# Weight and mask loads issued by SyncE or ScalarE, and a new order of work, in a kernel of attention and two expert layers

## The chip, the cores and the metric

One core of a Trainium2 chip runs the program. The metric is device time in microseconds from start to end of one execution; three runs give a median. One more execution was taken with the hardware profiler; all rows below come from that one.

## What is computed

Two batches of 8 heads, 768 positions, head size 64. Every position belongs to the cluster (of 16) whose centroid it is most alike; a query sees only keys of its own cluster. The attention output goes, as 1536 rows of 512, through two expert layers.

```python
q_assign = np.argmax(np.einsum('bhsd,hcd->bhsc', q_n, c_n), axis=-1)      # q_n, k_n, c_n: normalized
k_assign = np.argmax(np.einsum('bhsd,hcd->bhsc', k_n, c_n), axis=-1)
mask = q_assign[:, :, :, None] == k_assign[:, :, None, :]
scores = np.where(mask, scale * np.matmul(q, k.transpose(0, 1, 3, 2)), -1e9)
attn = softmax(scores); x = np.matmul(attn, v)        # -> (1536, 512)
h = x @ w_in                                          # 512 -> 2048
g = np.where(h >= 1, h, np.where(h <= -1, 0.0, (h + 1) ** 2 / 4.0))
x = g @ w_out                                         # 2048 -> 512
out = ((x @ w1) * (x @ w2)) @ w3 @ w_out2             # 512 -> 1024 -> 512
```

## The kernel before

Matmuls run on pairs of float32r numbers: each operand is split into a high part (a copy, L352 on ACT or L354 on DVE) and a low part (a subtraction, L357 on DVE or POOL), and three products are added (tiles of weights: `wf` whole, `whl` or `wh` split). The weights come as float64, seen as pairs of 32-bit words in a staging tile `w64`; L1107 and L1111 (ACT) and L1115 and L1121 (DVE) turn them into float32 in `wf`. Weights that batch 1 needs again are stored in DRAM (`wd`, L1126) and fetched from there.

The work has three stages. **Batch 0's attention** (about 0 to 200 us): keys and queries are loaded into `kq0` (L513), projected on the centroids (L539), turned into a mask of 16 rows per head (L555 to L590), and the mask rows are copied behind each head's keys and queries in `kq2` (the mask fill, L728). Beside it the product of the last two weight matrices is made (L1169) and kept in DRAM as `wp`. **The middle** (about 200 to 470 us): batch 1's attention beside batch 0's pass through the expert layers (L1239, 12 matmuls to a group of one weight tile and half the rows). **The last third**: batch 1's pass, for which sums and differences of blocks are made (L1403) so that seven products (L1492) do the work of eight.

Attention goes by units (two heads of one batch) and half units of 6 score tiles. A score tile is four matmuls (L859) into a bank `sc`; a maximum (L867, DVE), a bias (L872, POOL), the exponential (L880, ACT); then it must be transposed. In batch 0 PE does that (L897); in batch 1, except for two tiles, a high and a low half go to a `phl` buffer (L352 or L354, then L357) and a transposing DMA from SP's queue (L927) writes them to `pt`. There are two banks and two `phl` buffers in batch 1: a bank is free once the low half is made, a `phl` buffer once the DMA has landed. When the six tiles of a half unit are in `pt`, 36 matmuls (L976; L968 in batch 0) multiply them with the values.

The order is not found by a scheduler at run time. Every piece of work is declared with `add(name, {engine: cost}, due, ...)`, with alternatives such as `{"ACT": .., "DVE": (.., LATE)}`; a search made offline has chosen the order and the engine of each piece, and the string `ORDER` (two letters to a piece, 3035 pieces) holds the result. Each engine gets its instructions in that order and executes them in it. Instructions that issue DMAs stand in the same order: SP's are those of pieces declared with the engine "DMA", ACT's stand between its activations. Costs and due times in `add` are used by the search alone.

Before the change all 152 weight fetches (`load`, L1101, L1103 and L1413) and batch 0's seven mask fills (L728, two DMAs each) are issued by ACT; everything else by SP. In the middle stage `w64` has three buffers; a fetch into one waits until L1121 has read it.

Of the kernel before, what the change touches and what calls it, by code (L numbers as in the profile page):

```python
# [38 lines left out]
    "###*#,#0#%#(#8$V%X%[#.#2#4$0$.$6$2$X%e%h$8$:#F%V%b$<%c%q%k%m$Z$_$a%i%]$>$c$4$H#D$J#R#g%y&,:m:|%_#Z$%$(;0;>$@"  # L39
    "$B$F%|&#$e$L$g$N$]$q$i$k$s$P$m$o%s%u$u$w#>:q:o$,#J#L#B#_#:$D%o;#$R#q%w;L;%$T;4;2)u)w)y#y#c#<#N#T$*#u#V$y$|)|"  # L40
    ";@;B:s;(:u:x:y*4*(***,*6;**#*%#P#]*@*B%#;P;]*.*8*:*D*F;N#k#o#m#6#e#|#s#X*0*<*2*>;6;-;8;m;/&&;;;<;a*L*H$#*N*P"
    "<#*X*Z*];D;F&)*J*R#i#w#H#@#a*u;_;c;R*_*e<4;T;I;J+(*T*V*a*c*w+4+6+*;e;g;q;V<D<(*m;o;s*y*|+#+@&1*g+8+:;u+,+.<T"
    "+0+<&6<%&*+B+&+2<H*i*l*o&2&:+L+N;w;z+X+Z<*<,*r<.*s%>&5&9<X;X;Z+D&G+F+P+R+H+T<c+>+]+_+u&/&<+J+a+V+c;j;k%%+w+y"
    ",(,4,6&E,*<8<6<F<:<V+|<J<L+e<s<<&I<N%@&K<?,8,:,,,.<@+m,#,%<g,<,0,2,>,L,@,B,D+g,N,P<w=*,X,Z,]&N<e<i,F,R<k<Z<]"
    "<n<`<a<p=:;|<0<2,_,T,H,J,V&>+i+l,a,u,w,y<u<y<|=.=J=#%(,c&P-(-*-,+o<B<Q<R,|-#,e,g=>=,=<=0+q=X&@-.&B-4-6-8=@=B"
    "&M=2=D=i-%-:=5=6+s<q=%=(-0-2-<-@&c-B-D=N=L=P=R&S=U=V=Z=]=_&T=y->>0=k-F-L-X-Z-]-N,m,i=a,l-P=m=o=q=s=d=e>@-R-_"
    ">P=|>#>2&Y-H-u-w,o-e-g>%-J>a,q=8=G=H>(,s>4-a-T-V.(.*-d&Z>6-y=g=v=w>o-|>*>-&b>8>:%*>D&i&V&_>T&k&v>B>F>H&^>K>M"
    "&e.#.%-m-i.4.6.,..?#>s.@-k>e.0.3&o.8.B&m.D&g-o>.>=>>.:?4>R>V>c>q&s.L.N.P.X.<>X>Z.Z%B?(-q>N.F>g>i.R.>?F>u>l>w"
    "?%?*>z?,.H>n>~.T.]._.a.J?V.u.V-s>]/(/4?.?0/*/,.c?i&z(&?@>_/@/B.w?2?B?D&w($(-%,?8&q?y.m?Z?J/.?6?H?X&|((%D/6.y"
    ".|/#/8/:/<?m/%?:?<?>?L?]/D?N?_?k?o?a(..e/0/2?q/>%.%0%2%4%F?P.g?R/F?s/L/N/H/P?c@,@2@#@B?|%6%H/J(*/R@T?T?e?g%J"  # L50
    "%L/X%8%:%</Z.i.k.o?u@%@(@6@4@8/T0(/V/]/_.q.s@:?w@.@0@e/a/c/u@*0*0,@D@F@<@w@X/w@>0./y/|@i@V@g@N%N0406@H@J@L@Z"
    "/m/e@]00%P%R%T@kA.@`@m@o0#0%@|02080:@@@P@b@yA#A%@R@q0@0<0L0>/g/i0XA@AP/k0N0P0B0DA:/o0u0w0yA)@c@s@u0Z0R0F0T/q"
    "0H0KA*A2A0A40|0W0]0_0e0gA6ADAcABA,A<A>0a0cA8As/s1((0(2ARATAFAHAJ1*1,1.1#Ag(4(61416AVAXAe1%AMAiAkA]AZ0mAuAnAp"
    "100i1X1Z12B%Aw0kB,0o181:1@1L(:1N1P1B1D(=(8(>ANA_AaAy(AA|B#1R0q1<1]1T1>1F(B1_B/(E(H(M1e1g(NAqB(B*1H1J1V1a1d0s"
    "1i1kBJ2*2,(F(J2.Bi2022C.B01u1w1y1|(Z(P24(R1m(TBMBO1o2#2%26(V(X2(1q1sB2B4282:2<B6CLCkBkBn2FB82H2>2AD02B2DB>BP"
    "B]B@BBBDC02J2L2O2PC2B:B<BRCNCQB_BbBTBF2T2V2X2ZBHC4C6FLC82]BVD>2cBcBY2eB[2R2_2aBoBq2g2i2kBtC:C<BfBgC>B|C#C&Bu"
    "FPBw2m2oCn3%C@CB3(D2C(CD3*3,CF3436By383.30Fe3:CHCpCKC_CRCT3B3<(_C+CaCWC,3>(hD53D(]32CX3F3@CcCe(bFiD@(c(eG#DL"
    "DZ3H3K2y3P3R3TD#D%CZC]D(3V3LD*3NChCqCs3Y3Z3]CuD,DBD6D:3mD<DOCwD9DQD^Cz3_(jDiG(3a3c3e2qE.3gELD`2s3o(t3q3sDDDG"
# [81 lines left out]
def cluster_attention_moe_kernel(  # L140
# [115 lines left out]
    def G():  # L256
        return blk_tile("G")
# [401 lines left out]
    def dma_of(b):  # L659
        return nc.sync.dma_start if b else nc.scalar.dma_start  # L660
# [52 lines left out]
    def kq_fill(u, h):  # L713
        def fn(e):
            b, j = units[u]
            hd = 2 * j + h
            dma = dma_of(b)
# [1040 lines left out]
```

## Time and profile before

| | |
|---|---|
| median of 3 runs | 721.11 us (721.01 to 721.91) |
| the profiled execution: its time | 723.58 us |
| the profiled execution: its span | 721.5 us |
| PE, DVE, ACT, POOL busy | 699.0, 618.2, 468.2, 290.9 us |
| mean granted clock of TensorE | 0.998 |
| moved by DMA | 122.36 MB: 62.18 MB on SP's queue (q1), 59.42 MB on ACT's (q10) |

PE is the engine to look at: its idle time in each stage, and for each wait the instruction that ended it. A wait is put down to what came last. SP and ACT issue DMAs; the DMA share is the mean busy share of 16 DMA engines, and it can read above 1 where packets of several transfers overlap.

### The profile page before, as it was taken

How to read it: one execution, taken by the hardware profiler on the slowest of the kernel's cores; microseconds unless marked ns; L12 is line 12 of the kernel's file. 1: busy time of each engine (PE TensorE's matmuls, PEld its weight loads, DVE VectorE, ACT ScalarE, POOL GpSimd, SP SyncE). 2: the span in 40 equal slices, each digit the busy share in tenths (PEclk: the TensorE clock that was granted, in tenths of full speed). 3: DMA queues.
4: the chain of work that ended last, by engine and by line, in shares of the span. 5: the costliest groups of instructions: out<-in, count | busy, mean ns of one | idle time of the engine just before them, and what ended most of it. 6: DMA issues, size and time to landing. Idle time of an engine off the chain costs nothing.

```text
span 721.5 us, 11974 instructions
## 1 busy us (share of the span) xinstructions
PE 699.0 (97%) x4173; PEld 631.2 (87%) x4173; DVE 618.2 (86%) x1080; ACT 468.2 (65%) x872; POOL 290.9 (40%) x359
## 2 busy tenths in 40 slices
PE   5999999999999999999999989999999999999998
PEld 2876776677799999999899988999999999999997
DVE  7999999989889998898999879568878869999940
ACT  7998999779786877977787656236764525543211
POOL 3344433221253454455321312317573426387510
PEclk9999999999999999999999999999999999999999
DMA  8357867777989998998989898673222122121122
GB/s 313 124 179 232 278 208 251 249 250 219 231 190 199 216 226 220 215 243 160 267 216 247 208 155 202 155 219 113 59 88 74 45 73 61 52 80 59 58 70 77
DMA packets 125644, 122.36 MB, mean 170 GB/s; under 512 B 83792, under 2 KB 92432, under 8 KB 125584
## 3 DMA queue, kind: packets, MB, share of 16 engines
q1 hardware_dynamic: 103024, 62.18, 36.2%
q10 hardware_dynamic: 22560, 59.42, 26.3%
q8 instruction: 33, 0.54, 0.3%
q14 instruction: 27, 0.22, 0.1%
HBM read 75.79 MB, written 22.28 MB: 136 GB/s over the span
## 4 chain that ended last, share of the span: by engine, by line
PE 71%; DVE 11%; DMA 7%; ACT 6%; issue 3%; POOL 1%; ACTq 0%; SPq 0%; DVEq 0%; POOLq 0%
PE mo L1239 33%; PE sc L1239 6%; PE sc L859 6%; PE sc L1492 6%; PE mo L1492 4%; PE mo L1169 3%; PE av L976 3%; PE sc L897 2%; PE av L968 2%; DMA pt<-phl 2%; PE av L1239 2%; DMA wf<-wp 2%; PE av L1492 1%; DVE tv L1403 1%; ACT P L880 1%
## 5 line engine op out<-in xcount | busy, mean ns | idle before, releaser
L1239 PE MATMUL mo<-X,whl 128*128 128x384 f32 x912 | 167.9, 338 | 0.0
L1239 PEld LDWEIGHTS mo<-X,whl 128*128 128x128 f32 x912 | 159.5, 189 | 1.7 <-DVE G L354 0.3
L1239 PE MATMUL mo<-G,whl 128*128 128x384 f32 x672 | 124.1, 339 | 0.0
L357 POOL TENSOR_TENSOR whl<-wf,whl 128x512 fp32r<-128x512 f32 x62 | 81.2, 1310 | 97.9 <-DVE whl L354 42.2
L1239 PEld LDWEIGHTS mo<-G,whl 128*128 128x128 f32 x672 | 118.2, 188 | 1.0 <-issue 0.6
L867 DVE TENSOR_REDUCE nm<-sc 128x1 f32<-128x768 f32 x96 | 90.0, 950 | 5.7 <-PE sc L859 5.2
L872 POOL TENSOR_SCALAR nm<-nm 128x1 f32<-128x1 f32 x96 | 34.6, 360 | 146.9 <-DVE nm L867 141.5
L352 ACT ACTIVATE whl<-wf 128x512 fp32r<-128x512 f32 x71 | 44.4, 627 | 46.0 <-PE mo L1239 26.2
L1111 ACT ACTIVATE w<-w,down 128x512 uint32<-128x512 uint32 x72 | 54.5, 763 | 8.4 <-DMA pt<-phl 3.9
L859 PE MATMUL sc<-k,q 128*128 128x512 f32 (+1 forms) x192 | 54.1, 363 | 5.7 <-DVE phl L357 2.6
L880 ACT ACTIVATE sc<-sc,nm 128x768 f32<-128x768 f32 x46 | 40.0, 870 | 20.6 <-POOL nm L872 19.8
L1115 DVE SCALAR_TENSOR_TENSOR wf<-wf,w 128x512 uint32<-128x512 uint32 x72 | 51.0, 714 | 2.3 <-ACT wf L1107 1.7
L1107 ACT ACTIVATE wf<-w 128x512 f32<-128x512 f32 x72 | 47.4, 671 | 6.3 <-POOL whl L357 3.6
L1121 DVE SCALAR_TENSOR_TENSOR wf<-w,wf 128x512 uint32<-128x512 uint32 x72 | 50.3, 702 | 1.1
L880 ACT ACTIVATE P<-sc,nm 128x768 f32<-128x768 f32 x50 | 44.8, 898 | 9.9 <-DVE nm L867 5.6
L859 PE MATMUL sc<-kq 80*128 80x512 f32 (+1 forms) x192 | 49.7, 341 | 0.0
L357 DVE TENSOR_TENSOR phl<-sc,phl 128x768 f16<-128x768 f32 x46 | 43.8, 952 | 3.2 <-ACT phl L352 2.6
L357 DVE TENSOR_TENSOR whl<-wf,whl 128x512 fp32r<-128x512 f32 x50 | 35.1, 704 | 10.1 <-ACT whl L352 9.4
L859 PEld LDWEIGHTS sc<-k,q 128*128 128x128 f32 x192 | 31.4, 190 | 13.5 <-ACT pt L352 4.2
L897 PEld LDWEIGHTS sc<-ident,P 128*128 128x128 f32 x300 | 33.5, 140 | 10.1 <-ACT P L880 7.2
L1239 PE MATMUL sc<-G,whl 128*128 128x384 f32 x228 | 42.0, 339 | 0.0
L897 PE MATMUL sc<-ident,P 128*128 128x128 f32 x300 | 39.7, 275 | 2.3 <-ACT P L880 2.1
(235 smaller groups left out, 1462.0 us busy)
## 6 DMA issues: line engine op xcount, KB each, us to landing
wf<-wd ACTq DMA_DIRECT2D x64, 256.0 KB, 2.8
w<-in_w_out_dram ACTq DMA_DIRECT2D x24, 512.0 KB, 4.2
wd<-wf SPq DMA_DIRECT2D x48, 256.0 KB, 3.4
w<-in_w3T_dram ACTq DMA_DIRECT2D x16, 512.0 KB, 4.0
w<-in_w_in_dram ACTq DMA_DIRECT2D x16, 512.0 KB, 4.5
w<-in_w_dram ACTq DMA_DIRECT2D x16, 512.0 KB, 5.1
wp<-wf SPq DMA_DIRECT2D x16, 256.0 KB, 3.0
wf<-wp ACTq DMA_DIRECT2D x16, 256.0 KB, 3.2
```

Of the source, the lines that this page charges most:

```text
L352: nc.scalar.activation(out=out, in_=in_, func=AF.Copy)
L357: (nc.gpsimd if e == "POOL" else nc.vector).tensor_tensor(out=out, in0=a, in1=b, op=ALU.subtract)
L859: nc.tensor.matmul(ps[:, n], q[0:n_rows, q0:q0 + 128], k[0:n_rows, n], start=first, stop=not first)
L867: nc.vector.tensor_reduce(out=nm, in_=T[("sc", b), s], axis=AX.X, op=ALU.max, negate=True)
L880: nc.scalar.activation(out=new(("P", b), s).rearrange("p n s -> p (n s)") if by_pe(s) else T[("sc", b), s], in_=T[("sc", b), s], func=AF.E ...
L897: nc.tensor.transpose(T[("sc", b), s][:, c], p[:, c], ident)
L1107: nc.scalar.activation(out=T["wf", i], in_=T[w64, i].bitcast(F32)[:, :, 1], func=AF.Abs, scale=float(2.0 ** -112))
L1111: nc.scalar.activation(out=lo, in_=lo, func=AF.Identity, scale=float(2.0 ** -29 - 2.0 ** -41), bias=down)
L1115: nc.vector.scalar_tensor_tensor(out=w, in0=w, scalar=3, in1=T[w64, i][:, :, 0], op0=ALU.logical_shift_left, op1=ALU.bitwise_or)
L1121: nc.vector.scalar_tensor_tensor(out=w, in0=T[w64, i][:, :, 1], scalar=0x80000000, in1=w, op0=ALU.bitwise_and, op1=ALU.bitwise_or)
L1239: nc.tensor.matmul(acc, w[:, a, k4 * 128:(k4 + 1) * 128], rhs(c, k4), start=(first and k4 == 0 and n == 0), stop=(last and k4 == 3 and n = ...
L1492: nc.tensor.matmul(ps, lhs(av, a, k), rhs(bv, c, k), start=k == 0 and n == 0, stop=k == 1 and n == 2,)
```

## The change

Each weight fetch and each mask fill of batch 0 is now a piece that may stand on SP or on ACT, with costs for the search, and `ORDER` is another one. In the code:

```diff
-    def dma_of(b):
-        return nc.sync.dma_start if b else nc.scalar.dma_start
+    def dma_of(e):
+        return nc.sync.dma_start if e == "DMA" else nc.scalar.dma_start
...
-                    ("k2", u, h), {"DMA": 1.95} if b else {"ACT": 0.3}, p - 6.0, kq_fill(u, h),
+                    ("k2", u, h), {"DMA": 1.95} if b else {"ACT": 0.3, "DMA": (0.9, 8.0)}, p - 6.0, kq_fill(u, h),
...
-                nc.scalar.dma_start(out=new("wf", i), in_=src)
+                (nc.sync if e == "DMA" else nc.scalar).dma_start(out=new("wf", i), in_=src)
...
-            add(("wl", i), {"ACT": 0.2}, t - 14.0, load, list(needs) + W_AFTER[i:i + 1], [(w64, i)], behind="w64", moves=((0.46, 1.8),))
+            add(("wl", i), {"ACT": 0.2, "DMA": (0.5, 8.0)}, t - 14.0, load, list(needs) + W_AFTER[i:i + 1], [(w64, i)], behind="w64", moves=((0.46, 1.8),))
...
-    "iqi#i%iXitiuiZi]i_iwiyi|"
+    "iiiZi^i_i#iqisi%iuiwiyi|"
```

L1101 (fetches of float64 weights) and L1413 (batch 1's fetches) change as L1103 does. By the new table 100 of the 152 fetches and all seven mask fills are on SP: 34 of 44 fetches before the first transposing DMA of the middle stage, 22 of the 47 up to the last one (before the change 46 stood there), 44 of the 61 behind it. The first fetches of keys (`kT`, by head pair) come in the order 0, 2, 1, 3, after 1, 0, 2, 3 before; the printed rows do not tell the pairs apart. The pieces are the same 3035, and PE's sequence is nearly the same.

Where batch 1's last unit but one is done, SP's queue had transposes of two half units (`pt`, from the two `phl` buffers) beside stores of weights (`wd`):

```order
L927 DMA_TRANSPOSE pt1_97<-phl1_112 128x12x128
L1017 DMA xd_84<-tmp_4370 128x384
L927 DMA_TRANSPOSE pt2_98<-phl0_111 128x12x128
L1126 DMA wd_85<-wf_4441 128x512
L927 DMA_TRANSPOSE pt2_98<-phl1_112 128x12x128
L1126 DMA wd_85<-wf_4374 128x512
L1126 DMA wd_85<-wf_4495 128x512
L927 DMA_TRANSPOSE pt0_96<-phl0_111 128x12x128
L927 DMA_TRANSPOSE pt0_96<-phl1_112 128x12x128
```

and now has, for the same six score tiles:

```order
L927 DMA_TRANSPOSE pt1_97<-phl1_112 128x12x128
L1101 DMA w641_114<-in_w12_dram 128x1024
L1126 DMA wd_85<-wf_4312 128x512
L1126 DMA wd_85<-wf_4373 128x512
L1101 DMA w642_115<-in_w12_dram 128x1024
L927 DMA_TRANSPOSE pt2_98<-phl0_111 128x12x128
L927 DMA_TRANSPOSE pt2_98<-phl1_112 128x12x128
L1101 DMA w640_113<-in_w12_dram 128x1024
L1126 DMA wd_85<-wf_4413 128x512
L1126 DMA wd_85<-wf_4482 128x512
L1126 DMA wd_85<-wf_4528 128x512
L927 DMA_TRANSPOSE pt0_96<-phl0_111 128x12x128
```

The three fetches of `w12` into `w640` to `w642` stood on ACT; now a transpose has one or two of them ahead of it on SP.

On PE, at the same place, the score tile in bank `sc_1917` was followed by one group of L1239, the next score tile (bank `sc_1916`), another group, and then L976:

```order
L859 MATMUL sc_1917<-kq_105 128x512
L859 MATMUL sc_1917<-kq_105 128x256
L1239 MATMUL mo_1912<-X_2080,whl 128x384 x12
L859 MATMUL sc_1916<-k_99,q_102 128x512
L859 MATMUL sc_1916<-k_99,q_102 128x256
L859 MATMUL sc_1916<-kq_105 128x512
L859 MATMUL sc_1916<-kq_105 128x256
L1239 MATMUL mo_128<-X_2080,whl 128x384 x12
L976 LDWEIGHTS vn
```

and now (the banks are numbered 1913 and 1912):

```order
L859 MATMUL sc_1913<-kq_105 128x512
L859 MATMUL sc_1913<-kq_105 128x256
L1239 MATMUL mo_1907<-X_2086,whl 128x384 x12
L1239 MATMUL mo_1908<-X_2086,whl 128x384 x12
L1239 MATMUL mo_128<-X_2086,whl 128x384 x12
L976 LDWEIGHTS vn
```

Three groups and the 36 matmuls of L976 now stand ahead of the next score tile, `sc_1912`.

On DVE, in the last third, from the last y sum (L1274) to the last low half of `BX`, before:

```order
L1274 TENSOR_TENSOR Yp<-Yp,mo_128 128x384
L1403 TENSOR_TENSOR tt_4941<-Yp 128x384
L357 TENSOR_TENSOR X_75<-Yp,X_75 128x384
L1403 TENSOR_TENSOR Yp<-Yp,tt_4940 128x384
L357 TENSOR_TENSOR whl<-wf,whl 128x512
L357 TENSOR_TENSOR BX<-tt_4941,BX 128x384
L357 TENSOR_TENSOR BX<-Yp,BX 128x384
L1403 TENSOR_TENSOR tt_4942<-Yp 128x384
L357 TENSOR_TENSOR BX<-Yp,BX 128x384
L1403 TENSOR_TENSOR ws_4949<-wf 128x256
L1403 TENSOR_TENSOR ws_4950<-wf,ws_4948 128x256
L357 TENSOR_TENSOR BX<-tt_4940,BX 128x384
```

and now:

```order
L1274 TENSOR_TENSOR Yp<-Yp,sc_5174 128x384
L357 TENSOR_TENSOR whl<-wf,whl 128x512
L357 TENSOR_TENSOR X_75<-Yp,X_75 128x384
L1403 TENSOR_TENSOR tt_4945<-Yp 128x384
L357 TENSOR_TENSOR BX<-tt_4943,BX 128x384
L1403 TENSOR_TENSOR ws_4951<-ws_4950,wf 128x256
L357 TENSOR_TENSOR BX<-Yp,BX 128x384 x2
L357 TENSOR_TENSOR BX<-tt_4940,BX 128x384
```

Eleven instructions followed the y sum there, now eight do; one sum of weights (`ws`) has moved behind.

## Rows read from the trace of the kernel before

**Rows 1.** The page's totals: busy us, share of the span, instructions.

```profile
PE 699.0 (97%) x4173; PEld 631.2 (87%) x4173; DVE 618.2 (86%) x1080; ACT 468.2 (65%) x872; POOL 290.9 (40%) x359
```

**Rows 2.** Busy time of each engine by stage, granted clock, DMA share, GB/s.

```profile
0.00:200.00 200.00, 185.67 (x1126) 136.69 (x1127) 183.82 (x301) 173.74 (x295) 67.44 (x100) 1.00 0.73 231
200.00:470.00 270.00, 267.36 (x1660) 251.25 (x1659) 238.09 (x385) 187.86 (x343) 103.40 (x126) 0.99 0.90 207
470.00:722.00 252.00, 245.97 (x1391) 243.22 (x1389) 196.34 (x396) 106.56 (x236) 120.08 (x134) 1.00 0.26 81
```

**Rows 3.** Timeline of PE, 428 to 433: start, us, instruction, idle before.

```profile
428.52 2.29 PE L1239 MATMUL mo<-X,whl 128*128 128x384 f32 x12
432.97 1.01 PE L859 MATMUL sc<-k,q 128*128 128x512 f32 x2 [2.16 <-DVE phl L357]
```

**Rows 4.** The chain that ended last, 418 to 433: start, us, what.

```profile
417.98 12.90 DMA pt<-phl
...
430.97 0.97 DVE phl L354
...
432.97 1.65 PE sc L859 x4
```

**Rows 5.** The page's DMA issues: count, median us from issue to landing.

```profile
pt<-phl SPq DMA_TRANSPOSE x46, 4.2
```

**Rows 6.** The transposing DMA of L927 that was issued at 423.17, and its landing.

```profile
L927 SPq DMA_TRANSPOSE pt<-phl x1: 4213/4213/4213, 423.2 to 423.2; - x1
DMA to landing us min/median/max: 13.0/13.0/13.0
```

**Rows 7.** Timeline of ACT and its issues, 417 to 432.

```profile
417.82 0.83 ACTq L1101 DMA_DIRECT2D w<-in_w_dram  x2
...
426.79 4.50 ACTq L1101 DMA_DIRECT2D w<-in_w_dram  x2
431.33 0.75 ACT L1111 ACTIVATE w<-w,down 128x512 uint32<-128x512 uint32 x1 [3.92 <-DMA pt<-phl]
```

**Rows 8.** Stretches of 2 us as in rows 2: the granted clock is third from the end.

```profile
431.00:433.00 2.00, 0.03 (x1) 0.03 (x1) 1.97 (x3) 0.75 (x1) 0.00 (x0) 0.93 1.65 142
433.00:435.00 2.00, 2.00 (x6) 1.81 (x7) 1.86 (x4) 0.40 (x1) 0.58 (x2) 0.50 0.69 185
435.00:437.00 2.00, 2.00 (x10) 2.00 (x10) 1.77 (x3) 1.89 (x5) 0.65 (x1) 0.72 1.09 414
```

**Rows 9.** The third and fourth load of L513 and their landings.

```profile
L513 SPq DMA_DIRECT2D kq<-in_kT_dram x2: 431/432/432, 2.2 to 2.7; - x2
DMA to landing us min/median/max: 5.9/6.2/6.4
```

**Rows 10.** Timeline of PE and of DVE at the start.

```profile
8.25 1.51 PE L539 MATMUL sc<-kq,cT 128*32 128x384 f32 x8 [2.11 <-DMA kq<-in_kT_dram]
...
9.82 0.58 DVE L555 STREAM_TRANSPOSE P<-sc 128x384 f32<-128x384 f32 x1 [1.33 <-PE sc L539]
```

**Rows 11.** Waits of PE and of ACT, 20 to 200: us in total, times, longest.

```profile
PE sc L859 <- ACT pt L352: 2.2, 6, 0.7
PE sc L897 <- ACT P L880: 2.1, 4, 0.8
...
ACT whl L352 <- issue: 0.4, 1, 0.4
ACT wf L1107 <- issue: 0.3, 1, 0.3
```

**Rows 12.** The page's groups of instructions: the weight copies on ACT.

```profile
L352 ACT ACTIVATE whl<-wf 128x512 fp32r<-128x512 f32 x71 | 44.4, 627 | 46.0 <-PE mo L1239 26.2
```

**Rows 13.** Timeline of PE and of DVE, 622 to 630.

```profile
629.94 0.61 PE L1492 MATMUL mo<-BX,wh 128*128 128x384 f32 x2 [0.88 <-DVE BX L357]
...
622.42 0.54 DVE L1274 TENSOR_TENSOR Yp<-Yp,mo 128x384 f32<-128x384 f32 x1
...
627.58 0.97 DVE L1403 TENSOR_TENSOR ws<-wf 128x256 f32<-128x256 f32 x1
```

More of the change, by code (lines that the diff above doesn't have):

```diff
@@ L44 @@
[L44 to L58, printed above, removed]
@@ new lines @@
+    "+B+.*g*i*l+8+:+<<H<%+0+2<8;w<X+L+N;z+X+Z*o<*&>;g&2<,*r&;<.;X+D+F+P&9*s;Z;j;k<t&7+R+T+H+]+_+>&/&<+u+a+J+V,(,4"
+    "+c+m&F<6<F&D+w+y+|,#,6,8,*,,,:<:,.,<<J+e<L<N&5<V<<=+<Z&I<?<@,%<g,0,2,>,@,L,B,D+g<e<w=;,N,P,F,R,X,Z,],_<]<i<k"
+    ";|<0<2<n<p<`<a&K=J,H,T,J,V,a+i+l,u,w<u<y<|=#-(-*+o=X<B<Q%@&O<R=.=,=0,c,y,|-#=j=N=<=>+q&P-,&@&B,e,g-4-6-.=@=B"
+    "+s&S=2=D-%-8-:=L=P=5=6<q-0-2=%&c=]&L=R=T=z-@-<-B=m->=Z=k-L-X-N=W-P-D,m-F>1=(>A-Z-]-_>#,i,k=|=_=a&l&U=o=d=q=e"
+    ",o-H-a-u-w&W&t>Q>2-R-e-g=s=8>%=G=H-J,q>D-T-V&o-c&^.(.*>4.,>(>+>T,s>6-y-|=g=u&e>b&`>p%(=w>8>:>->B&X?#&[&b%B%*"
@@ new lines @@
+    ".4.6.8>F>H&j&n.#.%...:-i-k-m-o>J>L.0.@.3.B.D&v>.>=>R>V&g>>.L.N.P?4-q>e>c?(>q>s>X>Z.F.X.<.R.Z.].>>N?G>g>u>i?W"
+    "._>w.T.H?%?*>l?,>z>n.J.V>]>_?.>~?1.u.a/(/4.c?@?8&y&|/*-s/,&q?6/@.w/B/D?Z&w?H((/.?j?m?X.y.|?z(&?2?B?D(-($%,%D"
+    "/6/8/:.e?:?<?>?]?_.m?J?L/#/%@3/<?k?o/0/2/>?N?P?R?a?q%.%0%2%4@#/F%F?s/L/N%6%H/H/J@6?c?T?e@C%J%L/P/R@,(+@U@e/X"
+    "%8%:?u.g.i.k/Z/]?|.o(.@%@(@4/T0(@8@:?g?w@./V@*%</_.q.s/a/c@F@0@=@>@w/u/w/y0*0,@X@D@i/|040608/m0.000#@H@J%N%P"
+    "@V@g/e/g@Z@N%R@LA/AA%T0%020:@]@_@k@m@o@b@@@P@y@|A#0<0L0>0@0B/i/k0DA20N0P@q0F@RA%A(A*0R0X/oA0AQ0u0w0Z0]A:@c@s"
@@ L96 @@
+    "gTgCfefifmh%h*g>fggLh:h,g|fZh<h>g2gJhfhhhih.h1fohHhJfqgVgXhLh$fkfsgNhBh(h@h2fufwh6gZg_hNg]hkhpi)hqh8hsh4gPga"
+    "gigchDhmhTi*hXh[i3i5iDgeggi7i,i.i0hFh]i8huhPhVhRglh_hbhwgmhch|iGiHi>i;iOibiQici@iBiRhyilifiLiJinipigiTiViXi<"
+    "iiiZi^i_i#iqisi%iuiwiyi|"
 )
@@ L716, in fn @@
             hd = 2 * j + h
-            dma = dma_of(b)
+            dma = dma_of(e)
             kq2 = f(T[("kq2", b), (u, h)])
@@ L1100, in load @@
             if is64:
-                nc.scalar.dma_start(out=new(w64, i), in_=src.bitcast(U32).rearrange("p (n t) -> p n t", t=2))
+                (nc.sync if e == "DMA" else nc.scalar).dma_start(out=new(w64, i), in_=src.bitcast(U32).rearrange("p (n t) -> p n t", t=2))
             else:
-                nc.scalar.dma_start(out=new("wf", i), in_=src)
+                (nc.sync if e == "DMA" else nc.scalar).dma_start(out=new("wf", i), in_=src)
         def absv(e):
@@ L1151, in chunk @@
         else:
-            add(("wl", i), {"ACT": 0.2}, t - 12.0, load, needs, [("wf", i)], behind="wf", moves=((0.46, 1.05),))
+            add(("wl", i), {"ACT": 0.2, "DMA": (0.5, 8.0)}, t - 12.0, load, needs, [("wf", i)], behind="wf", moves=((0.46, 1.05),))
             last = ("wl", i)
@@ L1412, in load @@
             def load(e, i=i, n=n):
-                nc.scalar.dma_start(out=new("wf", i), in_=wd[n])
-            add(("wl", i), {"ACT": 0.2}, t - 16.0, load, [("wd", n)], [("wf", i)], behind="wf", moves=((0.46, 1.05),))
+                (nc.sync if e == "DMA" else nc.scalar).dma_start(out=new("wf", i), in_=wd[n])
+            add(("wl", i), {"ACT": 0.2, "DMA": (0.5, 8.0)}, t - 16.0, load, [("wd", n)], [("wf", i)], behind="wf", moves=((0.46, 1.05),))
             rows_.append(i)
```

85 lines of the change are left out of this document (44 added, 41 removed).

## The prediction, made before the result was known

> **What bounds the kernel now.** I read the page's totals first, then the span by stage, then TensorE's own waits, and last the chain through the one long wait. The totals [rows 1] say that PE is busy 699.0 of 721.5 us: whatever the change does to queues, PE's work stays, and what it can win is PE's idle time, what little the clock loses, and gaps too short to be listed. The stages [rows 2] say where that time is. Attention of batch 0 (0 to 200 us) leaves PE idle 14.3 of 200 us, the start among them; DVE (183.8) and ACT (173.7) are almost as full as PE there, so that stage has three engines near their limit. The middle (200 to 470: attention of batch 1 beside the first pass through the experts) leaves 2.6 us idle, with the DMA engines at 0.90. The last third (470 to 722) leaves 6.0 us, the end of the kernel among them.
>
> The 2.6 us of the middle are nearly one event. In PE's timeline [rows 3] a score matmul of L859 starts at 432.97 after 2.16 us of idleness. The chain [rows 4] tells why: a transposing DMA issued at 417.98 took 12.90 us to land; only then was its source buffer (one of two phl) free for the copy on DVE at 430.97, then came the subtraction that frees the score bank, then the matmul. The page's median for these transposes is 4.2 us [rows 5]; the next one, issued at 423.2, needed 13.0 [rows 6]. Beside the first, ACT's queue had just issued two weight loads of 512 KB (417.82), and at 426.79 two more issues took 4.50 us in which ACT itself stood still for 3.92 [rows 7]. The wait cost more than its length: the granted clock was at 0.50 in 433 to 435 and at 0.93 and 0.72 on either side [rows 8], that is 0.14 + 1.00 + 0.56 = 1.7 us of full clock lost, after an idle stretch of PE. Price of the event: 2.16 + 1.7 = 3.9 us.
>
> **The change, part by part.** It removes no arithmetic: 152 loads and 7 mask fills are issued as before, 100 of the loads and all fills now by SP. All else is order and the choice of engine for some copies and subtractions.
>
> *Issues that leave ACT.* Where ACT is busy an issue costs it nothing that the trace shows: in the whole stretch 20 to 200 us, with over 40 issues, ACT waited 0.7 us for "issue" [rows 11]. So the move itself is worth 0 to 0.7 us in batch 0's stage, and up to 3.92 us of ACT's time at 427, where ACT is not what PE waits for. I take 0. What is queued behind: on SP the transposes, stores and fetches now stand behind loads.
>
> *The long wait at 432.* Two things change there. First, PE's order: before, one group of 12 L1239 matmuls stood between the score matmuls that ended at 428.52 and those that waited; now three groups stand there, then the 36 matmuls of L976, and only then the score matmuls. A group is 2.12 us (the 12 from 428.52 end at 430.81 with their tail [rows 3]), so PE has 4.2 us more work before it needs anything late. But L976 needs the transposes of its own half unit, the one issued at 423.2 among them, which landed at 423.17 + 13.0 = 436.2. PE would reach L976 at 430.6 + 4.2 = 434.9: if the DMA engines behave as before, PE still idles 1.3 us, a gain of 0.9. Second, the loads: of the 46 loads between the first and last transpose of the middle stage, 22 move to SP's own queue, where they stand between transposes (31 of 49 transposes have none before them, 14 have one, 4 have two). On one queue transfers land one after the other: at the start, four 384 KB loads issued 0.47 us apart landed 0.96 us apart (2.19 + 5.93 = 8.12, 2.66 + 6.42 = 9.08 [rows 9]). If the late landings come from loads on the other queue beside a transpose, half of these are gone and the event with them: a gain of 3.9. Ends 0.9 and 3.9; neither row is nearer, so the middle: **-2.4 us**. Late next would be the L976 group of the last half unit, whose cover shrinks from seven L1239 groups after the last score matmul to six.
>
> *The start.* The table now fetches the keys in the order 0, 2, 1, 3 (before 1, 0, 2, 3). The first projection (L539) needs keys 0 and 1. Before, it began at 8.25 when the third load landed, and DVE waited 1.33 us for it [rows 10]. Now key 1 is the fourth load: 9.08. A quarter of the projection (the part on key 0, about 0.4 of its 1.5 us) can run first, so it ends 0.96 - 0.4 = 0.6 us later; DVE's next op waits for that, and DVE is dense behind it. **+0.6 us**, between 0 (if the stage is bound by ACT) and 1.0.
>
> *Batch 0's stage.* By the table's choices up to the first score of batch 1, DVE takes over two subtractions and gives up six shorter copies and subtractions, and ACT has four copies more. Two of the four are weight copies at 627 ns [rows 12]; at that length for all of them, an estimate, ACT has 2.5 us more to do and DVE as much less as it gains, so about 0. ACT has 26 us of slack in 200 [rows 2], but PE's longest waits there are for ACT, 2.2 and 2.1 us [rows 11]. So the term lies between 0 less the short gaps that a better order may close (4.3 us, a rival below) and +2.5; the slack is ten times the load, so I take **0**.
>
> *The last third.* PE idles 0.88 us at 629.94, before a product of L1492, for the last of the low halves of BX. DVE began the last y sum ahead of it (L1274) at 622.42 and had 11 instructions after that one, 7.5 us in all, two of them sums of weights at 0.97 [rows 13]. In the new order 8 stand there, one of them a sum of weights; at the mean of the old ones, (629.94 - 622.42) / 12 = 0.63 us, that is 5.6 us for nine, 1.9 less, while PE has six products in front, as before. So that wait goes: **-0.9 us**, between 0 (if the y sum itself comes later) and -0.9.
>
> Sum: -2.4 + 0.6 + 0 - 0.9 = -2.7 us. The profiled execution took 723.58 us, its span 721.5 with 2.1 around it; the median of the runs is 721.11. I put the difference on the median: **718.4 us** (720.9 for a profiled one).
>
> **Rivals.**
> *It makes no difference that can be measured* (within 0.2%, 1.4 us, about the least that runs of this kernel can tell apart). The late transposes come again whatever queue the loads use, since the same bytes pass the same 16 DMA engines: then -0.9 + 0.6 - 0.9 = -1.2, **719.9 us**. For it: the DMA share is 0.90 over the whole middle stage [rows 2]. Against it: transposes elsewhere land in 4.2 us at that same share. The Trainium skill ("DMA: Bandwidth & Descriptors", "Issuing engines are not separate DMA queues") says that DMAs of all issuing engines end on the same 16 DMA engines and interleave, so that another issuer saves only the sequencer's time; by that rule this rival is the whole story. The trace agrees on ACT's side; no row of it shows a transpose with the loads on its own queue.
>
> *Slower: SP's queue becomes the wait.* SP works in order. A load waits there until its staging buffer (w64, three of them in this stage) has been read by DVE; a transpose behind it waits too, its phl buffer stays full, and the score bank stays taken. The place is the middle stage, where every second or third transpose now has a load in front. One more event like that at 432 costs 3.9 us. The point from which it decides: the transpose that landed after 12.90 us cost 2.16, so up to 12.9 - 2.2 = 10.7 us cost nothing. From 4.2 that leaves 6.5 us; loads that merely pass in front, at 0.96 x 512/384 = 1.3 us each, would have to be five in a row, and there are at most two. So it takes a buffer wait of about 5 us. With the -2.4 gone too: 721.1 + 3.9 + 0.6 - 0.9 = **724.7 us**.
>
> *Slower: the first stage pays.* The 2.5 us more on ACT come straight on PE's waits for it: 721.1 + 0.6 + 2.5 - 0.9 = **723.3 us**, with the event at 432 unchanged.
>
> *Faster by more.* The order closes the gaps of batch 0's stage that PE spends on ACT, 4.3 us: 718.4 - 4.3 = **714.1 us**. For it: that stage has the most idle time. Against it: ACT has more to do there, not less.
>
> **How the numbers follow.** Forecast 0.38 (its own spread 716.9 to 719.9 by the ends 0.9 and 3.9), no difference 0.20, SP's queue 0.17, first stage 0.10, faster by more 0.15. Faster by over 0.2% means under 719.7: 0.35 of the forecast and the 0.15, together 0.50; within 0.2%: 0.20; slower: 0.17 + 0.10, and 0.03 of the forecast's share, for small losses somewhere in a thousand moved rows that outweigh it, 0.30. The range, 713.5 to 725.0, takes in all the cases and cuts off what lies beyond the last two.
>
> **What would show it.** Right: no idle stretch of PE over 1.5 us and no half clock between 400 and 450 us; fewer transposes that land after more than 6 us; the first L555 on DVE about 0.6 us later; no PE wait for BX. Wrong: SP waits of 5 us or more that end in a transposing issue and a PE wait for phl behind them; PE idle in 20 to 200 us well away from 5.6; or a stall at a place that is quiet now, which a new order can make anywhere.

## The result, and the profile after

The changed kernel took **714.4 us** (median of four runs, 713.39 to 715.43) against 721.18; the ratio is 0.990, 95% interval 0.988 to 0.992. It is 6.8 us faster, where 2.7 were forecast: inside the range near its lower end, on the right side, 2.5 times the size. In a later comparison it took 713.1 (ratio 0.989, 0.986 to 0.992), just outside the range.

The totals of the page after, and the stages as in [rows 2]:

```profile
PE 695.7 (98%) x4171; PEld 630.5 (89%) x4173; DVE 615.5 (86%) x1088; ACT 466.6 (66%) x877; POOL 276.5 (39%) x346
```

```profile
0.00:200.00 200.00, 187.64 (x1134) 138.29 (x1137) 182.85 (x298) 175.91 (x301) 65.04 (x100) 1.00 0.71 231
200.00:470.00 270.00, 270.00 (x1687) 255.05 (x1686) 236.41 (x385) 189.74 (x348) 105.96 (x124) 1.00 0.88 214
470.00:722.00 252.00, 238.06 (x1354) 237.19 (x1352) 196.21 (x407) 101.00 (x231) 105.50 (x122) 1.00 0.24 73
```

The middle, which left PE 2.6 us idle, leaves it nothing now, and the clock stays at 1.00. The last third ends at 711.6: 241.6 us, of which PE is busy 238.06, so 3.5 us idle, all of it behind the last matmul. Before, 251.5 us (the span ends at 721.5, the row at 722) with 245.97 busy leave 5.5, of which 3.5 are behind the last matmul and 2.0 are waits. Batch 0's stage has 12.4 us idle after 14.3.

To see where the time goes, the two traces were laid beside each other by PE's work: every matmul counted at the usual spacing of its kind, and the two times compared at which the same work was done. The changed kernel leads by 1.6 us at 200 us of the old time, 2.6 at 420, 6.3 at 450, 6.6 at 620 and 9.7 at the end. So two places carry it: the long wait at 432 (3.7) and the stretch from 620 to 685 (3.1). These two executions differ by 9.9 us (spans 721.5 and 711.6), more than the medians do: the first lay 2.5 us above its median, the second 0.9 below.

At the place of the long wait, PE's timeline after [rows 3], and the transposing DMA that has the place of the one that took 12.90 us [rows 4]:

```profile
424.86 0.51 PE L859 MATMUL sc<-k,q 128*128 128x512 f32 x2
425.21 0.52 PE L859 MATMUL sc<-kq 80*128 80x512 f32 x2
425.56 6.53 PE L1239 MATMUL mo<-X,whl 128*128 128x384 f32 x36
432.02 3.12 PE L976 MATMUL av<-pt,vn 128*64 128x384 f16 x36
435.06 0.62 PE L859 MATMUL sc<-k,q 128*128 128x512 f32 x2
```

```profile
L927 SPq DMA_TRANSPOSE pt<-phl x1: 1275/1275/1275, 418.8 to 418.8; - x1
...
DMA to landing us min/median/max: 4.3/4.3/4.3
```

Three groups (36 matmuls) and L976 follow each other without a gap. Of the 46 transposes of L927, 4 landed after more than 6 us, where 9 did before. The last third, in stretches that begin at the same product: before from 604.6 (the first stretch up to there), after from 598.0, columns as in [rows 2]:

```profile
472.20:604.60 132.40, 132.40 (x755) 131.99 (x754) 107.45 (x223) 70.12 (x151) 66.73 (x74) 1.00 0.31 94
604.60:630.00 25.40, 24.41 (x138) 23.75 (x136) 24.88 (x45) 11.99 (x28) 11.69 (x12) 1.00 0.15 42
630.00:660.00 30.00, 29.35 (x165) 28.71 (x166) 29.36 (x60) 12.85 (x33) 23.26 (x29) 1.00 0.24 71
660.00:690.00 30.00, 29.67 (x168) 28.94 (x167) 27.85 (x58) 7.11 (x17) 17.10 (x20) 1.00 0.17 53
```

```profile
465.70:598.00 132.30, 132.30 (x756) 132.30 (x755) 116.50 (x242) 65.18 (x146) 53.43 (x62) 1.00 0.30 91
598.00:621.50 23.50, 23.50 (x135) 23.50 (x134) 19.97 (x41) 10.94 (x25) 10.59 (x11) 1.00 0.16 45
621.50:651.00 29.50, 29.46 (x169) 29.14 (x168) 28.92 (x63) 14.52 (x36) 21.40 (x28) 1.00 0.26 81
651.00:681.00 30.00, 30.00 (x172) 29.77 (x171) 26.26 (x54) 7.45 (x18) 17.49 (x21) 1.00 0.22 71
```

DVE is the third busy column. Before, it was nearly full from 604.6 on (24.88 of 25.4, 29.36 and 27.85 of 30.0), and PE's listed waits there came from behind DVE's queue: 0.88 us for BX [rows 13] and 0.57 for G directly, 0.31 for a low half that POOL made late, since POOL itself had waited 2.22 us for a copy on DVE. PE's and POOL's timelines before:

```profile
650.00 1.31 PE L1492 MATMUL sc<-X,wh 128*128 128x384 f32 x6 [0.57 <-DVE G L357]
...
679.91 0.97 PE L1492 MATMUL av<-BX,wh 128*128 128x384 f32 x4 [0.31 <-POOL wh L357]
```

```profile
679.08 0.78 POOL L357 TENSOR_TENSOR wh<-ws,wh 128x256 fp32r<-128x256 f32 x1 [2.22 <-DVE wh L354]
```

After, DVE has room in two of the three stretches (19.97 of 23.5 and 26.26 of 30.0; 28.92 of 29.5 in the one between), and no wait of PE is listed from 200 us to the end. At the start the first L555 on DVE begins at 9.99 us, 0.17 later than before [rows 10]:

```profile
9.99 0.58 DVE L555 STREAM_TRANSPOSE P<-sc 128x384 f32<-128x384 f32 x1 [2.02 <-PE sc L539]
```

That comparison hides most of it, since the keys landed late in that execution of before. Over all traces the first L555 begins between 8.65 and 9.82 us with the old key order (nine traces) and between 9.98 and 10.47 with the changed one (four).

### The profile page after: what moved, and what is told of

The parts are those of the page before. It is cut to its first block, busy times and chain, and to the rows that moved or that the text cites. A ratio compares the mean times of both kernels' runs of the same rounds, so it can differ in the third digit from the quotient of the medians.

```text
span 711.6 us, 12019 instructions
## 1 busy us (share of the span) xinstructions
PE 695.7 (98%) x4171; PEld 630.5 (89%) x4173; DVE 615.5 (86%) x1088; ACT 466.6 (66%) x877; POOL 276.5 (39%) x346
## 4 chain that ended last, share of the span: by engine, by line
PE 85%; ACT 7%; DVE 5%; issue 2%; POOL 1%; DMA 0%; ACTq 0%; DVEq 0%
PE mo L1239 40%; PE sc L1492 9%; PE sc L859 7%; PE sc L1239 6%; PE mo L1492 6%; PE av L976 3%; PE mo L1169 3%; PE av L968 3%; PE sc L897 2%; ACT P L880 2%; PE av L1492 2%; DVE nm L867 2%; PE av L1239 2%; ACT pt L352 2%; ACT wf L1107 1%
## 5 line engine op out<-in xcount | busy, mean ns | idle before, releaser
L1239 PE MATMUL mo<-X,whl 128*128 128x384 f32 x912 | 167.1, 338 | 0.0
L1239 PEld LDWEIGHTS mo<-X,whl 128*128 128x128 f32 x912 | 158.7, 188 | 1.5 <-DVE G L354 0.3
L1239 PE MATMUL mo<-G,whl 128*128 128x384 f32 x696 | 128.9, 339 | 0.0
L1239 PEld LDWEIGHTS mo<-G,whl 128*128 128x128 f32 x696 | 122.4, 188 | 1.2 <-issue 0.3
L872 POOL TENSOR_SCALAR nm<-nm 128x1 f32<-128x1 f32 x96 | 32.3, 336 | 118.6 <-DVE nm L867 108.7
L352 ACT ACTIVATE whl<-wf 128x512 fp32r<-128x512 f32 x65 | 40.6, 627 | 34.4 <-PE mo L1239 7.8
L357 DVE TENSOR_TENSOR whl<-wf,whl 128x512 fp32r<-128x512 f32 x53 | 37.7, 713 | 3.6 <-ACT whl L352 3.2
L352 ACT ACTIVATE pt<-sc 128x768 f32<-128x768 f32 (+1 forms) x44 | 34.6, 810 | 5.2 <-PE sc L897 4.7
```

Of the source, the lines that this page charges most:

```text
L352: nc.scalar.activation(out=out, in_=in_, func=AF.Copy)
L357: (nc.gpsimd if e == "POOL" else nc.vector).tensor_tensor(out=out, in0=a, in1=b, op=ALU.subtract)
L1239: nc.tensor.matmul(acc, w[:, a, k4 * 128:(k4 + 1) * 128], rhs(c, k4), start=(first and k4 == 0 and n == 0), stop=(last and k4 == 3 and n = ...
```

## The experiments

All kernels below have the changed code; what differs is how the table is read. `read` turns a table into pairs of a piece and its choice of engine, `ORDER0` is the table of before, and a choice of 0 for a fetch (`wl`) or a mask fill (`k2`) of batch 0 is ACT, 1 is SP. Runs of before stood beside each group: medians 720.8, 721.3 and 721.1, single runs from 717.8 to 728.9.

**Order and issuers apart.** First the old order with the new issuers:

```diff
-    return read(ORDER)
+    by = dict(read(ORDER))
+    return [(i, by[i] if ops[i][0][0] in ("wl", "k2") else alt) for i, alt in read(ORDER0)]
```

> The order of before on all engines; only the issuers of the 152 fetches and of batch 0's mask fills are those of the changed table (100 fetches and all fills on SP). Theory Q (the queue: transposes land late when fetches from ACT's queue run beside them): the event at 432 us goes, 3.9 us: 721.2 - 3.9 = 717.3, no transpose of the middle lands after more than 8 us, PE idles under 0.5 us between 428 and 438. Theory O (the order alone does it, the issuer only says who writes the descriptor): 721.2, within 1 us, and late transposes of 10 us or more stay. Theory B (SP becomes the wait: a fetch that waits for w64 holds a transpose behind it): 724 or more, with SP waits of 5 us that end in L927 and PE waits for the low half of phl behind them.

Measured: 728.6 us, ratio 1.011 (1.008 to 1.015). Slower, but not where theory B had put it. By PE's work it is 8.2 us behind by 200 us and then gains 3.8 at the place of the long wait, which is gone. The loss is in batch 0's stage; waits of SP's queue up to 200 us (three rows), and the wait of PE at 17.96:

```profile
SPq L1126 <- DVE wf L1121: 24.9, 11, 5.9
...
SPq L1101 <- DVE wf L1121: 16.8, 6, 5.0
SPq L728 <- DVE mask L590: 9.9, 1, 9.9
```

```profile
17.96 1.18 PE L539 MATMUL sc<-kq,cT 128*32 128x384 f32 x6 [1.92 <-DMA kq<-in_qT_dram]
```

SP stands 9.9 us before a mask fill, with fetches behind it, and the last queries are late behind four weight fetches of 512 KB. Then the new order with the old issuers:

```diff
-    return read(ORDER)
+    return [(i, 0 if ops[i][0][0] in ("wl", "k2") else alt) for i, alt in read(ORDER)]
```

> The changed order on all engines, but every weight fetch and every mask fill of batch 0 issued by ACT again, at its place in the order. Theory O: 714.4, within 1 us of the changed kernel, and PE's idle time stays near 16 us. Theory Q: late transposes come back; with one event as at 432 in before, 714.4 + 3.9 = 718.3, and if the changed PE order covers most of it (4.2 us of work ahead of the late one), 714.4 + 1.3 to 1.3 + 1.7 of half clock: 716 to 717.4.

Measured: **765.3 us**, ratio 1.061 (1.056 to 1.066). No theory had that. It is 51 us over the changed kernel; by PE's work it is 24 us behind before by 200 us. ACT's timeline there, and PE's wait:

```profile
17.07 0.58 ACT L588 ACTIVATE mask<-sc,nbig 128x384 fp32r<-128x384 f32 x1 [3.92 <-PE sc L580]
17.17 0.38 ACTq L1101 DMA_DIRECT2D w<-in_w_out_dram  x1
...
21.36 0.67 ACT L1107 ACTIVATE wf<-w 128x512 f32<-128x512 f32 x1 [1.65 <-DMA w<-in_w_out_dram]
21.36 0.83 ACTq L1101 DMA_DIRECT2D w<-in_w_out_dram  x2
...
26.17 0.66 ACT L1107 ACTIVATE wf<-w 128x512 f32<-128x512 f32 x1 [3.49 <-DMA w<-in_w_out_dram]
```

```profile
30.40 1.01 PE L859 MATMUL sc<-k,q 128*128 128x512 f32 x2 [6.15 <-ACT mask L588]
```

On SP the first fetch of `w_out` went out early; in the changed kernel's SP timeline:

```profile
5.54 1.24 SPq L1101 DMA_DIRECT2D w<-in_w_out_dram  x2
```

On ACT the same piece stands behind a mask that waits for PE and goes out at 17.17; ACT then waits for its own fetches (1.65 and 3.49 us) with the masks behind them. So the order needs SP, as the old order needs ACT: neither half of the change is faster alone.

**By stage.** Both tables hold the same pieces, so one can be followed up to a piece and the other behind it. Old up to the last L976, then new:

```diff
-    return read(ORDER)
+    new, old = read(ORDER), read(ORDER0)
+    cut = [i for i, _ in old].index(names["pv", 7, 1])
+    done = {i for i, _ in old[:cut]}
+    return old[:cut] + [x for x in new if x[0] not in done]
```

> Order and issuers of before up to the last L976 product (469 us), those of the changed table behind it. If the last third is worth what the two profiles show (PE's matmuls, counted by work done, gain 3.4 us from 620 us on: at 629, 650, 658 and 680): 721.2 - 3.4 = 717.8. If only the wait for BX at 629.94 goes, as the prediction had it: 720.3. If the gain there comes from issuers or from work done earlier: 721.2.

Measured: 717.4 us, ratio 0.996 (0.994 to 0.998): 3.5 us gained, as read from PE's work and not as forecast. The last third is half of the result.

New up to batch 1's first score product, then old (the same code with the tables exchanged and the cut at `("s", 49)`):

> Order and issuers of the changed table up to batch 1's first score product, those of before behind it. If batch 0's stage is worth what the two profiles show (1.6 us by 200 us): 721.2 - 1.6 = 719.6, with the event at 432 still there. If that stage gives nothing, as the prediction had it (+0.6 for the start): 721.2 to 721.8. If stalls later move with it: anything, and then the middle of its profile must differ from that of before.

Measured: 720.9 us, ratio 1.001 (0.999 to 1.004): no gain that can be told. Its profiled execution took less (718.5) for another reason: the transpose that took 12.90 us took 10.6, though nothing in the middle had changed, and PE's long wait was not there:

```profile
L927 SPq DMA_TRANSPOSE pt<-phl x1: 1486/1486/1486, 417.0 to 417.0; - x1
...
DMA to landing us min/median/max: 10.6/10.6/10.6
```

In the run with the new last third the same transpose took 14.5 us, PE waited 3.8 us behind it, and the clock fell to 0.50 again:

```profile
PE sc L859 <- DVE phl L357: 4.3, 2, 3.8
```

So this event has another size in every execution. By PE's work up to 460 us, against executions in which PE does not wait there, it cost 3.8 us in the trace of before and 5.7, 0.1, 1.3 and 2.7 in the four other traces that keep the old order and issuers there: 2.7 in the mean. What one profile shows of it is no price.

**The event.** Of the two `w12` fetches that ACT issues at 417.8, beside the transpose, the second alone was moved: to SP, behind the transpose,

```diff
-    return read(ORDER0)
+    one = names["wl", 85]
+    return [(i, 1 if i == one else alt) for i, alt in read(ORDER0)]
```

> The kernel before with one thing changed: of its 152 fetches one, the second of the two w12 fetches that ACT issues at 417.8, is issued by SP, right behind the transposing DMA that landed after 12.90 us. In three executions of this order that transpose took 10.62, 12.90 and 14.51 us. Theory Q (a fetch from the other queue that runs beside a transpose delays it): the transpose lands in under 6 us, PE waits less than 0.5 us between 428 and 438, and the median falls by the mean price of the event, 2 us (median of before 720.8, its lowest runs, which I take for those without the event, 718.8): 718.8, with runs from 718.5 to 720. Theory S (the DMA engines are shared and it is the bytes in flight that delay): 720.8, the transpose again at 10 us or more.

or left on ACT and put behind the split of a weight (`whi`), five instructions later:

```diff
-    return read(ORDER0)
+    one, behind = names["wl", 85], names["whi", 83]
+    seq = [x for x in read(ORDER0) if x[0] != one]
+    at = [i for i, _ in seq].index(behind) + 1
+    return seq[:at] + [(one, 0)] + seq[at:]
```

> The kernel before with the same one fetch left on ACT, but issued five ACT instructions later, at about 421.7 us, when the transpose beside it should have landed (417.98 + 3.7). If it is the moment and not the queue: the first transpose lands in under 6 us and the median is 718.8, as with that fetch on SP. If the late fetch hits the next transpose (issued 423.2) instead: one of the two still lands after 8 us or more, 720 to 721. If neither queue nor moment matters: 720.8.

Measured: 719.0 us, ratio 0.997 (0.995 to 0.999), with SP; 718.4, ratio 0.996 (0.993 to 0.998), with ACT and later. One fetch of 152 wins 2.3 or 2.9 us, from SP as from ACT; the two intervals overlap. The runs (12 each) spread over 4.1 and 3.4 us, where the 23 of before beside them spread over 9.9. The transpose landed after 8.2 and 8.1 us, under the 10.7 that the prediction had worked out as free, and PE waits for nothing there:

```profile
L927 SPq DMA_TRANSPOSE pt<-phl x1: 1525/1525/1525, 419.7 to 419.7; - x1
...
DMA to landing us min/median/max: 8.2/8.2/8.2
```

```profile
L927 SPq DMA_TRANSPOSE pt<-phl x1: 1529/1529/1529, 418.9 to 418.9; - x1
...
DMA to landing us min/median/max: 8.1/8.1/8.1
```

That refutes theory Q, the queue, as it was stated (under 6 us), and leaves the number of fetches issued right beside the transpose: two in before (0.16 us ahead of it and 0.21 behind), one here. Both on SP:

```diff
-    return read(ORDER0)
+    two = [names["wl", 84], names["wl", 85]]
+    return [(i, 1 if i in two else alt) for i, alt in read(ORDER0)]
```

> The kernel before with both w12 fetches of 417.8 us issued by SP, behind the transposing DMA, the other 150 by ACT. With one of them moved the transpose still took 8.2 us, the other fetch beside it. If a fetch in the same queue behind a transpose doesn't hurt it (in ten traces 23 transposes with an SP fetch within 2 us behind or 1.5 ahead had a median of 3.77 us and none over 6): it lands in 3.7 to 4.5 us, but the fetch comes 1.7 us later than ACT issued it and ACT's conversion with it; 718.5, and no PE wait over 0.5 us there. If bytes in flight alone count: 8 us or more again, 719 all the same, as 8.2 us cost nothing.

Measured: 719.5 us, ratio 0.997 (0.996 to 0.999). The transpose took 5.3 us, between the two theories' numbers, and no more is gained, since what lies under 10.7 is free. The two fetches now go out 1.5 and 2.5 us behind it. Queue and moment are not parted by this: no run issues both from ACT at that later moment.

```profile
L927 SPq DMA_TRANSPOSE pt<-phl x1: 1462/1462/1462, 417.1 to 417.1; - x1
...
DMA to landing us min/median/max: 5.3/5.3/5.3
```

**The last third.** Is it the order or the issuers? As the run that gave 717.4, but with the fetches behind the cut on ACT:

```diff
-    return old[:cut] + [x for x in new if x[0] not in done]
+    return old[:cut] + [(i, 0 if ops[i][0][0] == "wl" else alt) for i, alt in new if i not in done]
```

> Order of before up to the last L976, the changed order behind it as in the run that gave 717.4, but with every fetch behind that point issued by ACT, as in before. If the last third's gain is DVE's order (DVE has 12 us more of its work in 470 to 600 and 8.5 us less in 600 to 690, where it was 96% busy): 717.4 within 0.7. If it needs the fetches on SP (weights that come early enough for DVE to work ahead): 720.8 or worse, since ACT gets fetches at places where they wait for a buffer; over 721 if ACT stands still there.

Measured: 732.3 us, ratio 1.014 (1.010 to 1.019). Here too the new order needs its fetches on SP. On ACT they come late, and the chain to PE is short; DVE's and PE's timelines:

```profile
485.02 0.42 DVE L1403 TENSOR_TENSOR ws<-wf 128x256 f32<-128x256 f32 x1 [4.50 <-DMA wf<-wd]
```

```profile
513.58 1.65 PE L1492 MATMUL mo<-X,whl 128*128 128x384 f32 x4 [3.24 <-POOL whl L357]
```

The run with the old order and the new issuers gained nothing behind 470 us by PE's work (it lost 0.5), so the issuers alone are not it either. Then, where in the order does it lie? The stretches above suggest a lead: DVE does 116.50 us of work ahead of the product at 604.6 instead of 107.45. With the cut moved to that product (`("y", 1, 3, 0, 0)`), DVE should come there with the old backlog:

> Order and issuers of before up to the product L1239 that starts at 604.6 us, the changed ones behind it; by that point both orders have issued the same pieces but one. If the last third's gain is DVE's lead (107.5 us of its work done in the 132.3 us ahead of that product in before, 116.5 in the changed kernel, so that it is 98% busy behind it in before and 85% in the changed one): DVE is as late as in before, nearly all of the 3.4 us stays lost, 720 to 721. If it is the order of the instructions on DVE from 622 to 630, as the prediction had it: at least 0.9 is gained, 720.2 or less, and 717.5 if that order is all of it.

Measured: 717.0 us, ratio 0.995 (0.993 to 0.997). My theory of the lead falls: the gain is there without most of it. The stretches of this kernel:

```profile
472.20:604.60 132.40, 132.40 (x754) 132.00 (x754) 108.85 (x226) 71.23 (x156) 67.88 (x76) 1.00 0.29 91
604.60:630.00 25.40, 25.40 (x146) 25.22 (x144) 22.26 (x46) 11.26 (x26) 11.02 (x12) 1.00 0.19 52
630.00:660.00 30.00, 29.96 (x171) 29.83 (x171) 29.06 (x61) 12.47 (x31) 24.50 (x31) 1.00 0.27 81
660.00:690.00 30.00, 30.00 (x173) 29.94 (x172) 24.76 (x53) 7.34 (x18) 13.56 (x17) 1.00 0.19 62
```

DVE came with 108.85 us done, 1.4 more than before where the changed kernel has 9.05 more, and still has 6.0 us less to do from 604.6 to 690 (76.1 after 82.1). The number of its instructions is nearly the same (160 after 163); they are shorter. In the slow place of before, POOL worked on sums of weights beside DVE's own [rows 13]; POOL's timeline before, and the same kind of sum on DVE after:

```profile
627.32 0.95 POOL L1403 TENSOR_TENSOR ws<-ws,wf 128x256 f32<-128x256 f32 x1
628.22 0.92 POOL L1403 TENSOR_TENSOR ws<-wf 128x256 f32<-128x256 f32 x1
```

```profile
621.47 0.41 DVE L1403 TENSOR_TENSOR ws<-wf 128x256 f32<-128x256 f32 x1
```

0.97 us beside POOL, 0.41 without. Summed over DVE's instructions from 604.6 to 690, what each took over the usual time of its kind, that is 9.2 us before, 3.4 with the cut at 604.6 and 3.8 in the same stretch of the changed kernel; nearly all of it is in instructions that have one of POOL beside them. That the order keeps DVE and POOL apart is read from these traces; it was not tried by itself.

**Batch 0's stage.** The old order up to batch 1's first score product, the new one behind it:

> Order and issuers of before up to batch 1's first score product (about 190 us), those of the changed table behind it. If batch 0's stage is worth the 1.6 us that the two profiles show by 200 us: 713.1 + 1.6 = 714.7. If that stage gives nothing, as the run with only the new first stage let it seem (720.9 against 720.8): 713.1. The prediction's start term (the changed start loses 0.6) would make it 712.5.

Measured: **712.6 us** (711.6 to 713.7), ratio 0.989 (0.987 to 0.991). It is the lowest median of all, but not one that can be told from the changed kernel's: against before beside it each time, the changed kernel had 0.990 and 0.989. So the new first stage gives nothing that these runs can tell. The 1.6 us that one pair of profiles showed lies within what executions differ: by PE's work at 200 us, seven other traces with the old first stage lie from 2.2 behind the trace of before to 2.7 ahead of it, and the four with the changed one at 0.0 to 1.6 ahead.

**The changed kernel again, and two edits.**

> The changed kernel once more, for its spread: 714.4, runs between 713 and 716. If the event at 432 is gone and not only smaller by chance, the runs spread over less than half of what those of before do (718.8 to 725.1), and no transpose of the middle lands after more than 8 us.

Measured: 713.1 us (712.85 to 715.05, six runs). The spread is 2.2 us, where that of before beside it (23 runs) was 9.9; the slowest transpose took 7.4 us. What is left of the spread begins at the start: in its profiled execution (715.05) the keys landed 0.4 us later than in the other (713.49), a wait of 1.15 us for the second mask followed, and PE was 1.5 us behind from there to the end.

```diff
+    seq[k1], seq[k2] = seq[k2], seq[k1]
...
+    n = [i for i, _ in rest].index(names["sexp", 30]) + 1
+    return rest[:n] + [x for x in seq if x[0] in late] + rest[n:]
```

> The changed kernel with two edits: the first fetches of keys in the order 0, 1, 2, 3 (the first projection needs 0 and 1; key 1 came fourth and landed at 8.4 to 8.8 us), and at 123.4 us two conversions on ACT behind the exponential for which PE waits 1.46 us there. If both waits are what they seem: 713.1 - 0.7 - 1.2 = 711.2, and the second level of the changed kernel's times (715) is gone. If DVE, dense behind the start, or the late conversions take it back: 713.1.

Measured: 713.8 us (712.4 to 715.6), ratio 0.991 (0.989 to 0.993): nothing gained. The exponential came earlier and its wait fell from 1.46 to 0.26, but the next one, behind the moved conversions, then held PE for 1.23. A wait for a full engine moves; it doesn't go.

## Why the prediction was right in part

*The long wait at 432, -2.4.* Near in size, and that in part by luck: 2.3, 2.9 and 1.6 were measured with one or both fetches moved. The forecast was the middle between two ends, 0.9 and 3.9, both priced from one execution. What happened is the upper end, the event gone whole, at a mean price of 2.7 instead of 3.9. The cover of three groups, on which the lower end rested, was not needed: the transpose landed after 4.3 us. The bound of 10.7 us held (10.6 cost next to nothing, 11.8 and 12.6 a wait of 1.1 and 1.8, 14.5 one of 3.8). The fetches beside the transpose are shown as the cause in the old order, but "on its own queue" is not shown to be what helps. The Trainium skill ("DMA: Bandwidth & Descriptors", "Issuing engines are not separate DMA queues") says that DMAs of all issuers share the same engines and interleave; the runs with one fetch moved agree (8.2 us with SP, 8.1 with ACT). But the rival that I hung on that rule, no difference at all, doesn't follow from it: bytes that come at another moment are no longer beside the transpose.

*The last third, -0.9.* **This is the term that was mis-sized**: 3.5 us measured, 4.1 with the cut at 604.6. The step that failed is "So that wait goes: -0.9 us", with -0.9 as the most that could be won. It looked at one wait, counted the instructions ahead of it and bounded the gain by that wait. The rows of the stretch said more: DVE was busy 96% of 85 us, so PE's other waits there (0.57 at 650.00, 0.31 at 679.91, and pauses too short to be listed) were the same shortage. The 0.97 us of a sum of weights stood in [rows 13] and was taken for its length, without asking why. The 6.0 us of idle time in that stage held only 2.0 us of waits.

*The start, +0.6, and batch 0's stage, 0.* The start does lose: by PE's work at 50 us the four traces with the changed first stage are 0.6 to 2.1 us behind the trace of before, the seven others with the old one 0.1 to 0.7 ahead of it. By 200 us it has been made up, so the two terms together are nothing that can be told, where +0.6 was forecast. PE's waits for ACT there came to 4.4 us, after 4.3 before: nothing closed, nothing opened. So that the result lies at the 714.1 of the rival "faster by more" is chance; its mechanism did not come.

```profile
PE sc L897 <- ACT P L880: 2.6, 3, 1.5
PE sc L859 <- ACT pt L352: 1.8, 5, 0.7
```

*Issues that leave ACT, 0.* True of ACT's time, and beside the point. What an issue on ACT costs is its place: the fetch goes out when ACT gets there, and ACT's next conversion waits for it. The two runs that follow the new order with fetches on ACT, everywhere or in the last third, show it: 44 and 11 us over before. That SP's queue would become the wait did happen, in the old order, at the start and not in the middle.

The parts add up to -2.3 - 3.5 = -5.8 of -6.8. By PE's work another 0.5 to 1.1 us is gained between 200 and 420 in the four traces with the changed order there (the eight others with the old order lie between 1.6 behind the trace of before and 0.3 ahead), in gaps too small to try. No run changes the middle alone. In the later comparisons the gain was 8.2, and 8.5 with the old first stage, so up to 2 us of it have no part to which the runs assign them.

## What to carry to other kernels

Who issues a DMA and where it stands in the order are one choice: an order made for fetches on a compute engine loses when they go elsewhere, and the other way round, so test the two halves apart before believing either. When an engine is full for a stretch, price the stretch, not the one wait that is listed; its small pauses and the lengths of its own instructions beside another engine count too. Where an event depends on what happens to meet, one profile gives its place but not its price: take that from the medians of many runs.

## What the runs showed of the hardware

*A transposing DMA and what flies beside it.* Over all 14 traces, 644 transposes of L927, by the 512 KB fetches that were issued up to 0.5 us after it and had not landed 0.3 us after its issue:

| fetches in flight | transposes | median to landing, us | longest |
|---|---|---|---|
| none | 379 | 3.89 | 9.5 |
| one from ACT | 171 | 4.49 | 15.8 |
| one from SP | 47 | 4.54 | 6.9 |
| two from ACT | 42 | 7.41 | 14.5 |

(Five more had other mixes.) By the medians the number counts and the queue doesn't. The slowest do differ, which the table can't explain, since the rows stand at different places of the program: of the 171 with one from ACT 15 landed after more than 8 us, of the 47 with one from SP none. SP issues one DMA after the other, and a transpose's issue takes it 1.3 us at least (1.4 in the median of the changed kernel), so a fetch that SP issues behind it comes that much later.

*The clock.* After idle stretches of 2.16 and 3.8 us at the long wait PE was granted 0.50, the level of 1.2 GHz; after 1.1 and 1.8 us there it stayed at 1.00. The length of the listed wait doesn't settle it, though. In the run with one fetch on SP the clock fell after 1.15 and 0.66 us close together:

```profile
154.91 0.52 PE L954 MATMUL mo<-ident,tmp 128*128 128x128 f32 x3 [1.15 <-DVE wf L1193]
156.09 0.64 PE L859 MATMUL sc<-k,q 128*128 128x512 f32 x2 [0.66 <-ACT pt L352]
```

```profile
158.00:160.00 2.00, 2.00 (x7) 1.61 (x6) 2.00 (x4) 1.38 (x3) 0.20 (x2) 0.51 1.09 406
```

In the new order with the fetches on ACT it stayed at 1.00 after 2.44:

```profile
219.04 0.59 PE L859 MATMUL sc<-k,q 128*128 128x512 f32 x2 [2.44 <-issue]
```

```profile
220.00:222.00 2.00, 2.00 (x13) 2.00 (x13) 2.00 (x4) 0.75 (x1) 0.19 (x1) 1.00 1.10 287
```

The price is steadier than the condition: of the eleven falls in the 14 traces ahead of the kernels' ends, nine cost 1.7 us of full clock each, as the prediction had worked it out at 432, and two cost 3.4.

*DVE beside POOL.* In the trace of before, sums of weights of one kind (`ws` from two `wf`, 128x256) took 0.42 us on DVE with POOL idle (4 of 4), and from 0.42 to 0.97, 0.81 in the median, with a POOL instruction beside them (8). The Trainium skill ("SBUF — State Buffer", "SBUF: two separate sides") says that DVE with two SBUF inputs and GpSimd share a pair of ports that one of them holds for its whole instruction. The rows agree in the main: the sum of 0.97 us ends 0.28 us after POOL's own of 0.95 that began ahead of it. One of the eight took 0.42 all the same.
